# Cross-shaped window attention: the tiles that were scored twice become 16-bit words in three phases, and the work order is new

## Chip, core and metric

One NeuronCore of a Trainium2 chip runs the whole kernel. The metric is device time in microseconds (us); the time of the kernel before is the median of 3 runs, 1017.18 us (1016.98 to 1017.32). Engines are named as in the profile: PE is TensorE (matmul, with PEld its weight loads), ACT is ScalarE, DVE is VectorE, POOL is GpSimd, SP issues most DMAs.

## The reference

```python
qkv = jnp.einsum('bhwc,cd->bhwd', x, wqkv)          # x: 1 x 224 x 224 x 96
# first 48 channels: 28 horizontal windows of 8 x 224 = 1792 tokens
ah = _softmax(jnp.einsum('bqc,bkc->bqk', qh, kh) * scale, axis=-1)
oh = jnp.einsum('bqk,bkc->bqc', ah, vh)
# last 48 channels: the same over 28 vertical windows of 224 x 8 tokens
...
return jnp.einsum('bhwc,cd->bhwd', o, wo)           # o: both halves side by side
```

So there are 56 windows, each with 1792 x 1792 scores, and one exp for each score.

## The kernel before

**Tiling.** The windows go in 28 pairs P (14 horizontal, then 14 vertical). A pair has four chunks c of 512, 512, 512 and 256 queries, and 14 key blocks of 128. One tile is 128 keys x 512 queries of both windows of the pair, so 128x1024 scores in two PSUM banks; in the chunk of 256 queries two key blocks share a tile. That makes 49 tiles for each pair and 1372 in all. A tile is scored on PE (`qk_fn`, L670, or `s_fn`, L683), turned into exp(score) in one of the bf16 buffers `PT`, and then summed over its keys against V by PE (`pv_fn`, L696), which adds all tiles of a chunk up in one PSUM bank. A column of ones in V gives the softmax sum with it.

**Who makes the exp.** Most tiles go to ACT, one ACTIVATE each (L888). The rest, `p_seq`, is computed without ACT, in one of three ways, which a backlog rule in `step_dve` picks (L1189, L1190):

- *whole*: DVE copies the scores to an f32 buffer `qb` (L1191). POOL then takes four steps over it (L1108 to L1111).
- *stay*: three DVE passes over the scores, which stay in PSUM (L1192, L1205, L1213). POOL does nothing.
- *scored twice*: DVE makes a factor in `qb` (L1192) and gives the PSUM banks back; POOL squares it into `PT` (L1105); later PE scores the tile a second time and DVE adds the square to these scores (L1213).

**Other work.** PE projects K, Q and V of the next pair in small fills (L435, L481, L463) that DVE evicts; DVE takes each finished chunk out of PSUM (L1166); PE multiplies it by wo (L530, L566); DVE divides by the softmax sum (L537, L545, L573, L580), and in the vertical half POOL adds the stored horizontal part (L584), or DVE does both in one (L593). SP sends the rows out.

**What sets the order.** A planner in the kernel (`Sched`, `step_pe`, `step_dve`, `step_pool`) runs once in Python with fixed durations and writes down one instruction list for each engine. On the chip each engine works through its list in order and waits on semaphores. Rules by pair and chunk (`HOW`) say how many of a chunk's tiles leave ACT and how PE groups its work. ACT scores come from two PSUM sets (`SETS`), and from the third when the p tiles leave it free, so PE can be about one tile ahead of ACT. PE works in two modes: scores and output fills (mode A), and PV and projection fills (mode B); `pe_switch` counts a cost for each change. There are 16 `PT` and 6 `qb` buffers.

Of the kernel before, what the change touches and what calls it, by code (L numbers as in the profile page):

```python
# [8 lines left out]
U16 = mybir.dt.uint16  # L9
ACTF = mybir.ActivationFunctionType  # L10
# [6 lines left out]
SOFF = 140.0  # L17
# [3 lines left out]
NPT = 16  # L21
NQB = 6
# [9 lines left out]
D_TS, D_TW = 1.125, 1.28  # L32
L_SQ, L_TS, L_TW, LATE_TS = 1.96, 1.145, 1.43, 0.13
# [9 lines left out]
HOW = [  # L43
    ("032", 6, "2953291003432 2653291003432 2653291013432 3653291013434"),
    ("333", 11, "3653391013234 3653391013234 5684191017241 5664191017243"),
    ("344", 7, "5664181027243 5664181027243 5664181028223 5681181025223"),
    ("444", 6, "5681181025223 5681180025223 5681180025223 5681180025223"),
    ("444", 2, "3764140021423 3764240021423 3764260121423 5764260121223"),
    ("333", 11, "2382160013403 2382360013443 2a24191028322 2a24191028323"),
    ("333", 1, "2a24191018323 2a24191018333 3a24191008133 3824191008133"),  # L50
    ("333", 10, "3824191018333 3824190018333 3874190018433 3874190028433"),
    ("443", 4, "3874190028440 3874190028440 3853190028430 3853191024430"),
    ("434", 12, "3833191024430 3833191020230 3833191020230 3832191020240"),
    ("325", 5, "5852251021313 2721171113121 2413281038423 2413281009423"),
    ("444", 2, "4413281009431 4413281019131 4813281029131 5324251019342"),
    ("313", 11, "4a63260030213 4994190008032 3462191002341 3162191002341"),
    ("524", 12, "4562191002341 4562191006441 4563191006143 2a23170011403"),
    ("534", 0, "2a23170011401 3a23170011411 3a23170011414 3a23270116414"),
    ("433", 2, "5942160006420 2973160008411 2973160008441 2973160008441"),
    ("334", 10, "2593341023304 2914380019334 4643191009032 2412280129443"),  # L60
    ("233", 8, "2083141038412 3811171010220 5613180028441 4433381011434"),
    ("444", 4, "5722161037443 5722191037443 5724191027443 5724191024444"),
    ("333", 5, "5724191020404 3a82181025434 3a82181025414 4a82181025434"),
    ("334", 11, "4a12161025431 4a12161025231 4a12161125214 3a11161125214"),
    ("444", 11, "5764190008424 5764191008424 5764191008421 5764191018420"),
    ("533", 11, "5764191018430 5764191017430 5764191037430 5761191033430"),
    ("333", 11, "5761191035430 2263191205441 5673280004431 5473280004434"),
    ("334", 6, "5463280034444 3973340009320 4954180009121 4954180009121"),
    ("333", 7, "4954180005141 4954180005121 4954181005121 4954181005124"),
    ("434", 3, "4954181005123 2424150226241 2424150036241 2424151036211"),  # L70
    ("434", 6, "5743180003230 3961260009412 2241270105112 2241270000112"),
]
OFF = [[int(d) for d in k] + [0] for k, _, _ in HOW]
TAIL = [t for _, t, _ in HOW]
RULES = [[[int(d, 16) for d in r[:8]] + [(0.0, 0.03, 0.06, 0.1)[int(r[8])]] + [int(d) for d in r[9:]] for r in rs.split()] for _, _, rs in HOW]
# [3 lines left out]
class Sched:  # L79
# [13 lines left out]
    def deps(self, eng, reads, writes):  # L93
        d = set()
        for k in reads:
            for s, v in self.wr.get(k, {}).items():
                if not (s == eng and eng == "pe"):
                    d.add((s, v))
        for k in writes:
            if k[0] != "out":  # L100
                for s, v in self.wr.get(k, {}).items():
                    if not (s == eng and eng == "pe"):
                        d.add((s, v))
            for s, v in self.rd.get(k, {}).items():
                if s != eng or k[0] == "rc":
                    d.add((s, v))
        return d
# [56 lines left out]
def bass_standalone__window_attn_cswin__vision_kernel(  # L164
# [15 lines left out]
    NCH = 4  # L180
# [11 lines left out]
    with es:  # L192
# [23 lines left out]
        PT = [sb(f"PT{i}", [128, 1024], BF16) for i in range(NPT)]  # L216
# [65 lines left out]
        KC = [4.8125 / 128.0, 21.0]  # L282
        QC = [60.0, 32.0]
# [50 lines left out]
        pool_now(["one"], lambda e: e.memset(one_sb[:], 1.0), 0.12)  # L334
        pool_now(["woz"], lambda e: e.memset(woh[:], 0.0), 0.2)
# [278 lines left out]
        def dve_commit(item, t):  # L614
# [18 lines left out]
        tiles = {}  # L633
        act_seq, p_seq = [], []
        pv_left = {}
        for P in range(NP):
            for c in range(NCH):
                sz = CH_SIZES[c]
                step = 512 // sz
                groups = [list(range(k, k + step)) for k in range(0, NKT, step)]  # L640
                off = OFF[P][c]
                na = len(groups) - off
                for i, kts in enumerate(groups):
                    t = dict(P=P, c=c, kts=kts, q0=CH_Q0[c], qs=sz, kind="A" if i < na else "P")
                    tiles[(P, c, i)] = t
                    (act_seq if i < na else p_seq).append(t)
                pv_left[(P, c)] = len(groups)
# [41 lines left out]
        def pv_fn(t, slot, st, sp_, pb):  # L689
            b = t["P"] % 2  # L690

            def fn(e):
                for i, kt in enumerate(t["kts"]):
                    for w in range(2):
                        ca = w * 512 + i * t["qs"]
                        ins = e.matmul(bank(pb)[64 * w:64 * w + CA, 0:t["qs"]], lhsT=V_sb[b][:, w, kt, :],  # L696
# [19 lines left out]
        s2_q = []  # L716
        s1_q = []
# [94 lines left out]
        def queue_prep(P):  # L812
# [4 lines left out]
            a0 = pair_act0[P - 1]  # L817
            n = pair_act0[P] - a0 if P < NP else 0
# [5 lines left out]
        pair_act0 = {}  # L824
        for i, t in enumerate(act_seq):
            pair_act0.setdefault(t["P"], i)
# [53 lines left out]
        def issue_qka(t, s):  # L880
            tl = act_seq[ia[0]]
            slot = slot_free.pop(0)
# [6 lines left out]
                PT[slot][:], ps[:, 512 * SETS[s]:512 * SETS[s] + 1024], ACTF.Exp, scale=LN2 / 128.0),  # L889
                set_keys(s), pt_keys(slot), fresh=pt_keys(slot))  # L890
            pv_ready[(tl["P"], tl["c"])].append((tl, slot))
# [13 lines left out]
        def v_keys(b):  # L905
            return [("V", b, k0) for k0 in range(0, 2 * NKT, VS)] + ["vones"]

        def pv_cands(t):
# [12 lines left out]
            for it in pv_ready[pc]:  # L921
                tl, slot = it
                rt = S.ready("pe", pt_keys(slot) + v_keys(P % 2), [], LATE)
# [3 lines left out]

        def issue_pv(it, t):
            tl, slot = it
# [3 lines left out]
            if first:  # L933
# [7 lines left out]
            S.commit("pe", t, D_MM, L_PV, pv_fn(tl, slot, first, last, pb),  # L941
                     pt_keys(slot) + v_keys(b), [("bank", pb)],
# [3 lines left out]
            slot_free.append(slot)  # L946
            if tl["kind"] != "A":
# [6 lines left out]

        def p_before(i, tl):
            return (p_seq[i]["P"], p_seq[i]["c"]) <= (tl["P"], tl["c"])

        def how():
            tl = act_seq[min(ia[0], len(act_seq) - 1)]
            return RULES[tl["P"]][tl["c"]]  # L960

# [3 lines left out]
        def step_pe():  # L965
# [8 lines left out]
            def p_wants():  # L974
                return bool(s2_q and s2_q[0]["ready"] <= t + 0.2) or (n_mid() <= PBACK and p_open())

            def p_open():
                if ip[0] >= len(p_seq) or not qb_free or p_ahead[0] >= PAHEAD or not slot_free:
                    return False
                tl = p_seq[ip[0]]  # L980
# [381 lines left out]
```

## Time and profile before

| | |
|---|---|
| median of 3 runs | 1017.18 us |
| profiled execution, first to last instruction | 1015.7 us |
| ACT busy | 1004.9 us (99%) |
| PE busy (ends modelled) | 977.0 us (96%) |
| DVE busy | 956.6 us (94%) |
| POOL busy | 930.7 us (92%) |
| granted PE clock | 1.000 |

The profiled execution has no other time of its own than the span; the median of the runs is 1.5 us above it, which lies before the first and after the last instruction. In a list of groups, a line reads: line of the kernel, engine, operation, output <- input, shapes, count | busy us in all, mean ns of one | idle time ahead of it and what ended that. In a timeline: start us, duration us, engine, line, operation, count.

### The profile page before, as it was taken

What the parts mean: (1) busy time and instruction counts of PE and PEld (TensorE: products, weight loads), DVE (VectorE), ACT (ScalarE), POOL (GpSimd) and SP (SyncE); (2) the same over time, 40 slices, a digit from 0 to 9 for tenths busy, and PEclk for the clock granted to TensorE, in tenths of its full rate; (3) what the DMA queues carried; (4) which work ended last, traced back from release to release, by engine and by line L of the source; (5) the groups of instructions that cost most, each with busy time, mean ns of one, the idle gap of its engine ahead of it and who ended that gap; (6) DMA issues with size and microseconds to landing.
All of it is one profiled execution on the core that took longest, in us unless ns stands there. A gap on an engine that the chain in (4) does not pass through costs nothing.

```text
span 1015.7 us, 30751 instructions
## 1 busy us (share of the span) xinstructions
PE 977.0 (96%) x13367; PEld 392.0 (39%) x13367; DVE 956.6 (94%) x1468; ACT 1004.9 (99%) x1101; POOL 930.7 (92%) x717
## 2 busy tenths in 40 slices
PE   9999999999999999999999999999999999999997
PEld 4433434443433334333343433333433343343333
DVE  7989999999999999999999999999999999999997
ACT  8999999999999999999999999999999999999997
POOL 5999999989999998999999898999999999999995
PEclk9999999999999999999999999999999999999999
DMA  3222303202220320222022133122312213312111
GB/s 87 62 65 65 63 17 66 66 18 62 66 65 2 79 65 8 60 39 38 1 39 48 26 59 56 26 51 58 59 22 61 48 20 61 52 36 58 20 23 34
DMA packets 162873, 47.02 MB, mean 46 GB/s; under 512 B 155895, under 2 KB 162711, under 8 KB 162738
## 3 DMA queue, kind: packets, MB, share of 16 engines
q1 hardware_dynamic: 161618, 44.57, 22.0%
q8 instruction: 104, 1.70, 0.7%
q10 hardware_dynamic: 1120, 0.49, 0.2%
q14 instruction: 31, 0.25, 0.1%
HBM read 10.60 MB, written 19.28 MB: 29 GB/s over the span
## 4 chain that ended last, share of the span: by engine, by line
ACT 99%; PE 1%; DVE 0%; issue 0%; DVEq 0%
ACT PT L888 99%; PE ps L346 0%; PE ps L731 0%; DVE out_all L593 0%; ACT xT_sb L747 0%; DVE OT_sb L1166 0%; PE ps L696 0%; PE ps L670 0%; DVE warm L309 0%; DVEq L192 0%; PE ps L753 0%; DVE rc L573 0%; DVE scr L310 0%
## 5 line engine op out<-in xcount | busy, mean ns | idle before, releaser
L888 ACT ACTIVATE PT<-ps 128x1024 bf16<-128x1024 f32 x1090 | 1000.5, 1094 | 1.1 <-PE ps L670 1.1
L670 PE MATMUL ps<-QT_sb,KT_sb 49*64 49x512 bf16 (+1 forms) x5144 | 447.4, 363 | 31.0 <-ACT PT L888 17.0
L696 PE MATMUL ps<-PT,V_sb 128*49 128x512 bf16 (+1 forms) x3136 | 456.2, 361 | 0.9 <-ACT PT L888 0.5
L670 PEld LDWEIGHTS ps<-QT_sb,KT_sb 49*64 49x64 bf16 x5144 | 129.8, 103 | 374.3 <-ACT PT L888 355.5
L1109 POOL TENSOR_TENSOR PT<-PT 128x1024 f16<-128x1024 f16 x138 | 261.4, 1894 | 9.8
L1110 POOL TENSOR_SCALAR qb<-PT 128x1024 uint16<-128x1024 f16 x138 | 186.2, 1349 | 12.0
L696 PEld LDWEIGHTS ps<-PT,V_sb 128*49 128x49 bf16 x3136 | 133.6, 103 | 163.8 <-issue 131.6
L1192 DVE TENSOR_SCALAR qb<-ps 128x1024 f32<-128x1024 uint16 x144 | 175.9, 1222 | 7.2 <-PE ps L683 5.4
L1213 DVE SCALAR_TENSOR_TENSOR PT<-ps,PT 128x1024 uint16<-128x1024 bf16 x144 | 175.7, 1220 | 5.6 <-PE ps L683 5.1
L1191 DVE COPY qb<-ps 128x1024 f32<-128x1024 f32 x138 | 168.6, 1222 | 11.5 <-PE ps L683 10.3
L1108 POOL TENSOR_SCALAR PT<-qb 128x1024 f16<-128x1024 uint16 x138 | 144.5, 1047 | 33.7 <-DVE qb L1191 23.8
L1111 POOL TENSOR_SCALAR PT<-qb 128x1024 uint16<-128x1024 f32 x138 | 144.5, 1047 | 11.2
L683 PE MATMUL ps<-QT_sb,KT_sb 50*64 50x512 bf16 x1376 | 136.0, 385 | 1.7 <-DVE qb L1192 0.4
L1105 POOL TENSOR_TENSOR PT<-qb 128x1024 f16<-128x1024 f32 x62 | 116.0, 1894 | 1.0
L1205 DVE SCALAR_TENSOR_TENSOR PT<-ps,qb 128x1024 f16<-128x1024 uint16 x82 | 100.0, 1219 | 0.1
L584 POOL TENSOR_TENSOR out_all<-tmp,Ph_sb 128x480 bf16<-128x480 f32 (+1 forms) x73 | 74.4, 1032 | 3.3 <-DVE tmp L580 1.6
L1166 DVE CAST OT_sb<-ps 113x512 bf16<-113x512 f32 x112 | 69.3, 618 | 6.1 <-PE ps L696 5.4
L451 DVE CAST QT_sb<-ps 128x512 bf16<-128x512 f32 (+1 forms) x111 | 68.1, 616 | 5.1 <-PE ps L435 4.5
L440 DVE TENSOR_SCALAR_CACHE_REDUCE KT_sb<-ps 128x512 bf16<-128x512 f32 x108 | 66.3, 616 | 3.2 <-PE ps L435 2.5
L545 DVE TENSOR_TENSOR Ph_sb<-ps,rc 128x480 bf16<-128x480 f32 (+1 forms) x84 | 52.2, 621 | 2.0
L488 DVE CAST V_sb<-ps 128x480 bf16<-128x480 f32 (+1 forms) x84 | 51.9, 620 | 2.2 <-PE ps L481 1.7
L683 PEld LDWEIGHTS ps<-QT_sb,KT_sb 50*64 50x64 bf16 x1376 | 39.2, 104 | 31.1 <-DVE PT L1213 9.6
(64 smaller groups left out, 444.5 us busy)
## 6 DMA issues: line engine op xcount, KB each, us to landing
cols_dram<-in_x_dram SPq DMA_DIRECT2D x28, 336.0 KB
out_dram<-out_all SPq DMA_DIRECT2D x386, 24.0 KB, 1.9
xT_sb<-cols_dram SPq DMA_TRANSPOSE x28, 4.8
xT_sb<-in_x_dram SPq DMA_TRANSPOSE x26, 4.7
xT_sb<-ones_dram SPq DMA_DIRECT2D x26, 7.0 KB
Ph_sb<-in_x_dram SPq DMA_DIRECT2D x2, 168.0 KB, 3.5
Ph_sb<-in_x_dram ACTq DMA_DIRECT2D x2, 168.0 KB, 3.7
out_dram<-out_all ACTq DMA_DIRECT2D x6, 24.0 KB, 1.9
```

The costliest lines, as they stand in the source:

```text
L670: ins = e.matmul(bank(SETS[s] + w)[64 * kh:64 * kh + 64, i * t["qs"]:(i + 1) * t["qs"]], lhsT=KT_sb[b][64 * w:64 * w + CA, kt * 128 + 64 * ...
L683: ins = e.matmul(bank(PB0 + w)[64 * kh:64 * kh + 64, 0:512], lhsT=KT_sb[b][64 * w:64 * w + nr, kt * 128 + 64 * kh:kt * 128 + 64 * kh + 64] ...
L696: ins = e.matmul(bank(pb)[64 * w:64 * w + CA, 0:t["qs"]], lhsT=V_sb[b][:, w, kt, :], rhs=PT[slot][:, ca:ca + t["qs"]], start=st and i == 0 ...
L888: S.commit("act", 0.0, D_ACT, None, lambda e, s=s, slot=slot: e.activation(PT[slot][:], ps[:, 512 * SETS[s]:512 * SETS[s] + 1024], ACTF.Ex ...
L1105: return [("pool", (D_SQ, L_SQ, 0.0), lambda e: e.tensor_tensor(y, q, q, ALU.mult), qk, yk)]
L1108: return [("pool", (D_TS, L_TS, LATE_TS), lambda e: e.tensor_scalar(y, lo, 2.0 ** -16, QH, ALU.mult, ALU.add), qk, yk), ("pool", (D_SQ, L_ ...
L1109: ("pool", (D_SQ, L_SQ, 0.0), lambda e: e.tensor_tensor(y, y, y, ALU.mult), yk + ["pser"], yk),
L1110: ("pool", (D_TW, L_TW, LATE_TS), lambda e: e.tensor_scalar(lo, y, 65536.0 * P2, 65536.0 * QC0, ALU.mult, ALU.add), yk + ["pser"], [("q", ...
L1111: ("pool", (D_TS, L_TS, LATE_TS), lambda e: e.tensor_scalar(bits, q, 1.0, 128.0 * (127.0 - SOFF), ALU.mult, ALU.add), qk, yk)]
L1191: S.commit("dve", t, D_P1, D_P1 + SEMD, lambda e: e.tensor_copy(qb[tl["qb"]][:], ps[:, PB0 * 512:(PB0 + 2) * 512]) if tl["whole"] else e.t ...
L1192: qb[tl["qb"]][:], ps[:, PB0 * 512:(PB0 + 2) * 512]) if tl["whole"] else e.tensor_scalar(
L1213: S.commit("dve", t, D_P1, D_P1 + SEMD, lambda e: e.scalar_tensor_tensor(PT[tl["slot"]][:].bitcast(U16), half(BF16, 1), 128.0 * (127.0 - S ...
```

## The change

Tiles are no longer scored twice. The tiles that do not go to ACT now have a written kind, by pair and chunk, in `TYPES`: `w` (the four POOL steps as before, the last one now a plain copy that converts), `s` (the three DVE passes as before), and the new `p`. The rows of `TYPES` hold 124 `w`, 95 `p` and 81 `s`. For a `p` tile:

- PE scores it once. The scores carry the factor 128, so that as a 16-bit word they are the bits of a bf16 number, which rises in straight pieces between powers of two.
- DVE makes these words in one pass over PSUM, straight into a `PT` buffer (it adds a constant and converts).
- POOL makes two more tiles from it in one step: it reads pairs of words as int32 and adds 42 or 85 to each word, so the straight pieces are shifted by a third and two thirds of an octave.
- PE sums all three tiles, the two shifted ones against copies of V scaled by 0.793 and 0.637 (`VB_sb`, made by POOL, two small steps for each pair, for the last three key blocks alone).

So a `p` tile takes three `PT` buffers and three PV groups. There are 25 `PT` and 4 `qb` buffers now. All rules of the order are new (`HOW`: one for each half of a chunk's ACT tiles). The core of the diff:

```diff
-NPT = 16
-NQB = 6
+NPT = 25
+NQB = 4
...
-    ("032", 6, "2953291003432 2653291003432 2653291013432 3653291013434"),
+wps pwsp wwsp
+wws pwsp wwps
...
-        KC = [4.8125 / 128.0, 21.0]
-        QC = [60.0, 32.0]
+        KC = [4.8125 / 128.0, 4.8125]
+        QC = [1728.0, 127.0]
...
+            if g[0] == "V" and all(("V", g[1], k0) in flags for k0 in range(0, 2 * NKT, VS)):
+                b = g[1] % 2
+                for j in range(2):
+                    pool_q.append(dict(what="vb", P=g[1], j=j, reads=[("V", b, k0) for k0 in range(0, 2 * NKT, VS)] + ["vones", "pser"], writes=[("VB", b)],
+                                       fn=lambda e, b=b, j=j: e.tensor_scalar(VB_sb[b][:, j, :, :, :], V_sb[b][:, :, NKT - KPH:NKT, :], PH_W[j], None, ALU.mult)))
...
+            pv_left[(P, c)] = n + 2 * (len(kinds) - late)
...
-                        ins = e.matmul(bank(pb)[64 * w:64 * w + CA, 0:t["qs"]], lhsT=V_sb[b][:, w, kt, :],
+                        ins = e.matmul(bank(pb)[64 * w:64 * w + CA, 0:t["qs"]], lhsT=VB_sb[b][:, ph - 1, w, kt - (NKT - KPH), :] if ph else V_sb[b][:, w, kt, :],
...
-            if not tl["whole"]:
-                return [("pool", (D_SQ, L_SQ, 0.0), lambda e: e.tensor_tensor(y, q, q, ALU.mult), qk, yk)]
+            if tl["kind"] == "p":
+                a, b, c = tl["slots"]
+                words = PT_all[:, :, :].rearrange("p s n -> p (s n)").bitcast(I32).rearrange("p (s n) -> p s n", s=NPT)
+                return [("pool", (D_SQ, L_SQ, 0.0), lambda e: e.tensor_tensor(
+                    words[:, b:c + 1:c - b, :], words[:, a:a + 1, :].to_broadcast([128, 2, 512]),
+                    kph[:, :].unsqueeze(2).to_broadcast([128, 2, 512]), ALU.add), pt_keys(a) + ["pser"], pt_keys(b) + pt_keys(c))]
...
-                    ("pool", (D_TS, L_TS, LATE_TS), lambda e: e.tensor_scalar(bits, q, 1.0, 128.0 * (127.0 - SOFF), ALU.mult, ALU.add), qk, yk)]
+                    ("pool", (D_TS, L_TS, LATE_TS), lambda e: e.tensor_copy(bits, q), qk, yk)]
...
-                rt = S.ready("dve", pt_keys(tl["slot"]), [])
-                s2_q.append(dict(t=tl, ready=rt - 0.5))
...
+                if kind == "p":
+                    fn = lambda e: e.tensor_scalar(PT[tl["slot"]].bitcast(U16), sc, -PH_OFF, None, ALU.add)
+                elif kind == "w":
+                    fn = lambda e: e.tensor_copy(qb[tl["qb"]][:], sc)
```

How the instruction lists change, counted from both:

| engine | what | before | now |
|---|---|---|---|
| ACT | exp of a tile | 1090 | 1072 |
| PE | score groups for tiles off ACT | 344 | 300 |
| PE | PV groups of one tile | 1372 | 1562 |
| PE | changes from mode A to mode B | 773 | 896 |
| DVE | passes over 128x1024 | 508 | 462 |
| DVE | output in one (128x96) / by way of POOL | 53 / 73 | 185 / 45 |
| POOL | whole tiles, four steps each | 138 | 124 |
| POOL | squares / phase steps | 62 / 0 | 0 / 95 |
| POOL | output adds / steps for the scaled V | 73 / 0 | 45 / 56 |

The other fills, evictions and DMAs are the same in number. PE's list near the middle of the program, where chunks of a horizontal pair run, stood as follows (L670 scores for ACT, L683 scores for a tile off ACT, L696 PV, L530 an output fill; four score matmuls or two PV matmuls are one tile):

```order
L670 MATMUL ps<-QT_sb,KT_sb 64x512 x4
L683 MATMUL ps<-QT_sb,KT_sb 64x512 x4
L670 MATMUL ps<-QT_sb,KT_sb 64x512 x4
L530 MATMUL ps<-woh,OT_sb 64x97 x10
L696 MATMUL ps<-PT,V_sb 49x512 x4
L670 MATMUL ps<-QT_sb,KT_sb 64x512 x4
L683 MATMUL ps<-QT_sb,KT_sb 64x512 x4
L670 MATMUL ps<-QT_sb,KT_sb 64x512 x4
```

Now a like place, with the PV groups of a `p` tile in it (L728 scores for ACT, L754 PV, L472 a projection fill), reads:

```order
L728 MATMUL ps<-QT_sb,KT_sb 64x512 x4
L754 MATMUL ps<-PT_all,V_sb 49x512 x2
L754 MATMUL ps<-PT_all,VB_sb 49x512 x2
L728 MATMUL ps<-QT_sb,KT_sb 64x512 x4
L754 MATMUL ps<-PT_all,VB_sb 49x512 x2
L472 MATMUL ps<-xT_sb,wq_sb 64x512 x2
L754 MATMUL ps<-PT_all,V_sb 49x512 x2
L728 MATMUL ps<-QT_sb,KT_sb 64x512 x4
```

What moved: the score group of a tile off ACT stood between two ACT score groups without a change of mode; where PV groups took its place, nearly every ACT score group stands alone between two changes.

POOL's list in the early part stood so (L1108 to L1111 the four steps of a whole tile, L1105 the squares):

```order
L1109 TENSOR_TENSOR PT<-PT 128x1024
L1105 TENSOR_TENSOR PT<-qb 128x1024 x3
L1110 TENSOR_SCALAR qb<-PT 128x1024
L1111 TENSOR_SCALAR PT<-qb 128x1024
L1108 TENSOR_SCALAR PT<-qb 128x1024
```

Now, at a like place (L1184 to L1187 the four steps, L1176 the phase step, with `kph` the two constants):

```order
L1185 TENSOR_TENSOR PT_all<-PT_all 128x1024
L1176 TENSOR_TENSOR PT_all<-PT_all,kph 128x2x512
L1186 TENSOR_SCALAR qb<-PT_all 128x1024
L1176 TENSOR_TENSOR PT_all<-PT_all,kph 128x2x512
L1187 CAST PT_all<-qb 128x1024
L1184 TENSOR_SCALAR PT_all<-qb 128x1024
```

What moved: the squares, which came in runs, are gone, and phase steps stand between the four steps of the whole tiles.

More of the change, by code (lines that the diff above doesn't have):

```diff
@@ L9 @@
 U16 = mybir.dt.uint16
+I32 = mybir.dt.int32
 ACTF = mybir.ActivationFunctionType
@@ L73 @@
-OFF = [[int(d) for d in k] + [0] for k, _, _ in HOW]
-TAIL = [t for _, t, _ in HOW]
-RULES = [[[int(d, 16) for d in r[:8]] + [(0.0, 0.03, 0.06, 0.1)[int(r[8])]] + [int(d) for d in r[9:]] for r in rs.split()] for _, _, rs in HOW]
+TYPES = """
+wps pwsp wwsp
+wws pwsp wwps
+wws wpsp pwws
+wsw wpsp pwws
+wsw wpsp pwws
+wsw wpsp pwws
+wsw wpsp pwws
+wsw wpsp pwws
+wsw wpsp pwws
+wsw wpsp pwws
+wsw wpsp pwws
+wp wwspp pwss
+wp wwspp wwss
+wp wwspp wwss
+wp wwspp wwss
+wp pwwspp wss
+wp pwwspp wss
+w pwwpsp wss
@@ L634, in bass_standalone__window_attn_cswin__vision_kernel @@
         act_seq, p_seq = [], []
         pv_left = {}
[L636 to L647, printed above, removed]
+        GROUPS = [NKT, NKT, NKT, NKT // 2]
@@ new lines, in bass_standalone__window_attn_cswin__vision_kernel, with add_chunk @@
+        POS0 = [0, NKT, 2 * NKT, 3 * NKT]
+        NPOS = sum(GROUPS)
+        def add_chunk(P, c):
+            sz = CH_SIZES[c]
+            step = 512 // sz
+            kinds = OFFS[P][c]
+            assert step == 1 or not kinds
+            left = [list(range(k, k + step)) for k in range(0, NKT, step)]
+            n = len(left)
+            na = n - len(kinds)
+            late = sum(z != "p" for z in kinds)
+            rest = left[na:]
+            for z in kinds:
+                if z == "p":
+                    kts = rest.pop()
+                    assert kts[0] >= NKT - KPH
+                else:
+                    kts = rest.pop(0)
+                p_seq.append(dict(P=P, c=c, kts=kts, q0=CH_Q0[c], qs=sz, kind=z))
+            for i in range(na):
+                act_seq.append(dict(P=P, c=c, kts=left[i], q0=CH_Q0[c], qs=sz, kind="A",
+                                    pos=P * NPOS + POS0[c] + i * n / na, seg=2 * (4 * P + c) + (2 * i >= na), first=i == 0))
+            pv_left[(P, c)] = n + 2 * (len(kinds) - late)
```

246 lines of the change are left out of this document (141 added, 105 removed).

## Prediction

> **What bounds the kernel now.** I read the busy shares first, then the chain that ended last, then the waits, since four engines are above 90%.
>
> ```profile
> PE 977.0 (96%) x13367; PEld 392.0 (39%) x13367; DVE 956.6 (94%) x1468; ACT 1004.9 (99%) x1101; POOL 930.7 (92%) x717
> ```
>
> The shares alone name no bound. The chain in order of time does:
>
> ```profile
> 9.07 0.37 PE ps L670 x4
> 9.44 0.02 issue
> 9.46 810.43 ACT PT L888 x883
> 819.89 0.02 issue
> 819.91 190.05 ACT PT L888 x207
> 1009.96 0.04 issue
> ```
>
> From 9.46 to 1009.96 us the end is set by one exp after the other: 810.43 + 190.05 = 1000.5 us for 883 + 207 = 1090 tiles. The group and the waits say the same from the other side:
>
> ```profile
> L888 ACT ACTIVATE PT<-ps 128x1024 bf16<-128x1024 f32 x1090 | 1000.5, 1094 | 1.1 <-PE ps L670 1.1
> ```
> ```profile
> PEld ps L670 <- ACT PT L888: 355.5, 926, 0.8
> ```
>
> One exp costs 1000.5 / 1090 = **0.918 us** (the mean of 1094 ns counts the overlap with the next). ACT waited 1.1 us in all for scores, while PE's loads of score weights waited 926 times for ACT to give a PSUM set back. So a tile taken off ACT is worth 0.918 us, as long as the others keep ACT fed.
>
> **ACT's term.** The rows of `TYPES` leave ACT 1072 tiles instead of 1090: 18 x 0.918 = **16.5 us** less. The exp itself keeps its shape and its operands. The head (9.46 us) and the tail (1015.7 - 1009.96 = 5.7 us) keep their steps but for a few output rows; I take both as unchanged. With ACT never idle the span is 9.46 + 1072 x 0.918 + 5.7 = 999.2 us, and with the 1.5 us by which the median of the runs is above the span, 1000.7 us. The question is what the other three engines make of it.
>
> **PE's term.** Matmul ends are modelled, so I count from start to start, in stretches without a wait:
>
> ```profile
> 502.59 0.41 PE L670 MATMUL ps<-QT_sb,KT_sb 49*64 49x512 bf16 x4
> 502.83 0.39 PE L683 MATMUL ps<-QT_sb,KT_sb 50*64 50x512 bf16 x4
> ...
> 503.56 0.39 PE L530 MATMUL ps<-woh,OT_sb 49*64 49x97 bf16 x10
> 503.88 0.62 PE L696 MATMUL ps<-PT,V_sb 128*49 128x512 bf16 x4
> 504.43 0.41 PE L670 MATMUL ps<-QT_sb,KT_sb 49*64 49x512 bf16 x4
> 504.77 0.62 PE L696 MATMUL ps<-PT,V_sb 128*49 128x512 bf16 x4
> 505.31 0.41 PE L670 MATMUL ps<-QT_sb,KT_sb 49*64 49x256 bf16 x8
> ...
> 506.55 0.40 PE L696 MATMUL ps<-PT,V_sb 128*49 128x512 bf16 x2
> 506.78 0.38 PE L435 MATMUL ps<-xT_sb,wq_sb 97*64 97x512 bf16 x2
> 507.10 0.41 PE L670 MATMUL ps<-QT_sb,KT_sb 49*64 49x256 bf16 x8
> ```
>
> Score to score takes 0.24 us (502.59 to 502.83), score to PV 0.34: a change of mode costs 0.10. Two PV tiles and the way back take 0.54 (504.77 to 505.31), one PV tile alone about 0.22 (0.23 from 506.55 to 506.78), so the way back costs 0.10 too. A projection fill is 0.22 (506.78 to 507.10 less the change), an output fill of ten matmuls also 0.22 (503.56 to 503.88 less the change). A V fill is 0.31:
>
> ```profile
> 140.43 0.48 PE L481 MATMUL ps<-w_sb,xT_sb 96*64 96x48 bf16 x20
> 140.74 0.38 PE L696 MATMUL ps<-PT,V_sb 128*49 128x512 bf16 x2
> ```
>
> Before: 1434 score groups x 0.24 + 1372 PV x 0.22 + 773 pairs of changes x 0.20 = 801 us, and the fills about 104 (K and Q 168 x 0.22 and 56 halves, output 157 x 0.22, V 78 x 0.31): 905 us, 90% of the 1000.5 in which the exps run. After: 62 fewer score groups (-14.9), 190 more PV (+41.8), 123 more pairs of changes (+24.6): **956 us, or 97%** of 984. PE's cover shrinks from 95 to 28 us. As PE can be no more than about one tile ahead, what counts is the local load. I walk through both lists with these durations. In the old order 2 of 1071 stretches of 20 ACT tiles ask more than the 18.36 us that ACT takes for them, the worst 18.45; in the new order 49 of 1053 do, the worst 19.03. A score group must have ended (0.41 us) before ACT is through with the other set (0.918), so PE may be late by 0.4 to 0.5 us before ACT notices. Summing what goes over that reserve gives 0 in the old order, as the trace has it, and 2.7 to 4.2 us in the new; with a reserve of only 0.3 it gives 7. Bounds 0 and 7; I take **3.5 us**, in the middle of the sums nearest to the trace.
>
> **DVE's term.** All passes over a tile cost alike:
>
> ```profile
> L1192 DVE TENSOR_SCALAR qb<-ps 128x1024 f32<-128x1024 uint16 x144 | 175.9, 1222 | 7.2 <-PE ps L683 5.4
> L1213 DVE SCALAR_TENSOR_TENSOR PT<-ps,PT 128x1024 uint16<-128x1024 bf16 x144 | 175.7, 1220 | 5.6 <-PE ps L683 5.1
> L1191 DVE COPY qb<-ps 128x1024 f32<-128x1024 f32 x138 | 168.6, 1222 | 11.5 <-PE ps L683 10.3
> ...
> L593 DVE SCALAR_TENSOR_TENSOR out_all<-ps,rc,Ph_sb 128x96 bf16<-128x96 f32 x53 | 13.0, 311 | 0.3
> ```
> ```profile
> 703.83 0.66 DVE L580 TENSOR_TENSOR tmp<-ps,rc 128x480 f32<-128x480 f32 x1
> 704.41 1.21 DVE L1191 COPY qb<-ps 128x1024 f32<-128x1024 f32 x1
> 705.54 0.16 DVE L467 TENSOR_REDUCE wq_sb<-ps 96x2 bf16<-96x8 f32 x1
> ```
>
> A pass occupies 1.13 us (704.41 to 705.54), and f32, 16-bit, one or two operands are the same within 2 ns. So the new pass, f32 scores to 16-bit words, is priced the same, from these rows; its bounds are half and twice that, -54 to +107 us for 95. There are 46 fewer passes: -52 us. Of the output, 28 tiles of scaled rows fewer at about 0.58 (703.83 to 704.41) are -16, and 132 more one-row steps at 13.0/53 = 0.245 are +32. Sum -36: busy 921 us, 92% of the span. DVE gets looser, at the twice price it would not (1028).
>
> **POOL's term.**
>
> ```profile
> L1109 POOL TENSOR_TENSOR PT<-PT 128x1024 f16<-128x1024 f16 x138 | 261.4, 1894 | 9.8
> L1110 POOL TENSOR_SCALAR qb<-PT 128x1024 uint16<-128x1024 f16 x138 | 186.2, 1349 | 12.0
> L1108 POOL TENSOR_SCALAR PT<-qb 128x1024 f16<-128x1024 uint16 x138 | 144.5, 1047 | 33.7 <-DVE qb L1191 23.8 <-DVE rc L573 0.4
> L1111 POOL TENSOR_SCALAR PT<-qb 128x1024 uint16<-128x1024 f32 x138 | 144.5, 1047 | 11.2
> L1105 POOL TENSOR_TENSOR PT<-qb 128x1024 f16<-128x1024 f32 x62 | 116.0, 1894 | 1.0
> L584 POOL TENSOR_TENSOR out_all<-tmp,Ph_sb 128x480 bf16<-128x480 f32 x47 | 51.1, 1097 | 2.2 <-DVE tmp L580 1.0
> L319 POOL COPY wq_sb<-wst 96x96 bf16<-96x96 bf16 x4 | 1.1, 264 | 0.2
> L327 POOL COPY w_sb<-wst 96x192 bf16<-96x192 bf16 x1 | 0.3, 341 | 1.7 <-DMA wst<-in_wqkv_dram 1.7
> ```
>
> A whole tile is 1.894 + 1.349 + 2 x 1.047 = 5.34 us busy; 14 fewer are -75. The 62 squares go, -116; 28 adds go, -29. Two copies, 264 ns for 96 elements and 341 for 192, give 0.8 ns an element: 1.0 us for 1024, so the converting copy in place of L1111 is priced at L1111's 1.05; and 0.42 for the 294 of a scaled V: 56 x 0.42 = +24. The unknown is the phase step, int32 words, 1024 results, two inputs, one of them read twice. No row has int32. Two-input steps take 1.894 with f16 and with f32 inputs alike, which speaks for the element count as the price. Bounds: 1.05, as a one-input pass of 1024, and 3.79, as if each of the 2048 16-bit words were an element. I take 1.9, the row nearest in count and inputs: 95 x 1.9 = +180. Sum -16: 915 us busy. The gaps between POOL's steps come on top (idle ahead of L1109, L1110 and L1111 is 33 us for 414 steps, 0.08 each; with L1108, less the 24 us in which it waits for DVE, some 45 to 50 us in all): before 930.7 + 50 = 981, after about 915 + 48 = 963 us, **96% of the span** as before. So POOL has little to spare, and the phase step decides.
>
> The Trainium skill (GPSIMD Engine Reference, section 3.1) gives a two-input elementwise step on GpSimd about 2.6 cycles an element at 1.2 GHz. That would be an estimated 2.2 us for 1024 elements, 29 us more in 95 steps; the trace has 1.894 for both two-input rows, so by the trace the page's figure is too high here, and whether int32 behaves as f32 does no run shows.
>
> What the change adds in waits: PV of the two shifted tiles waits for POOL, and behind it in PE's list stand ACT's next scores. DVE's pass for a `p` tile frees the score banks after 1.13 us, where a scored-twice tile took them twice; that is in DVE's favour. DMAs are the same in number.
>
> **The sum.** 9.46 + 984.0 + 3.5 + 5.7 = 1002.7 us of span, and 1.5 outside: **1004 us**.
>
> **Rivals.**
>
> 1. *ACT stays fed*: the order has PE lean just where ACT has a tile in hand. For it: 1.1 us of waiting in 1000 now, with POOL as full. Against it: 97% of PE. It gives 1000.7 us.
> 2. *PE is held by POOL*: a phase step of 2.2 us brings POOL to 991 us with its gaps, 99% of the span. Each of the 95 then lands late for a PV group whose successors are ACT's scores; if a third of the 0.3 us excess passes ACT's reserve it costs 95 x 0.1 = 10 us: 1010 to 1015 us. For it: one or two phase steps stand between the steps of whole tiles, so their results come late too.
> 3. *POOL becomes the bound, and the kernel slower*: without phase steps POOL's sum is 963 - 180 = 783 us; with a step of x us, 783 + 95x. It passes the 1000.5 us that the exps take now at x = 2.3, and since POOL then sets the end, the time is above 1017 from about there (head and tail as they are). At the upper bound, 3.79, it is 1143 + 15 + 1.5 = 1160 us. For it: int32 is in no row, and the output is 4 bytes wide. Against it: f32 input of 4 bytes costs nothing over f16.
>
> **How the numbers follow.** Forecast (some PE stalls, 1002.5 to 1009) 0.43; rival 1 (999.5 to 1002.5) 0.27; rival 2 (1009 to 1015) 0.13; between that and no change within 0.2%, 1015.1 to 1019.2, which is about what a measurement of this kernel can tell, 0.05; rival 3 0.12. Faster is 0.43 + 0.27 + 0.13 = 0.83. The range takes in the forecast, rival 1 and most of rival 2: 999.5 to 1014, which holds 0.81. PE's bounds (0 and 7 us of stalls) lie in it; the upper bounds of DVE's pass and POOL's step are what is left out.
>
> **What would show it.** Right: 1072 exps at 0.918 us; idle ahead of them of 2 to 7 us, ended by PE's scores; far fewer waits of PE's score weights for ACT than 355 us; phase steps near 1.9 us; DVE busy near 921. Wrong: a phase step above 2.2 us, POOL without idle time and PE's PV waiting for it (rival 2 or 3); or ACT idle above 10 us with POOL on time, which would mean that changes of mode cost more in the new order than 0.20 a pair.

## The result and the profile after

The changed kernel takes **1008.38 us** (median of 4 runs, 1008.03 to 1008.55), against 1017.08 us (1016.88 to 1017.32, 4 runs) for the kernel before. The ratio is 0.9914, 95% interval 0.9900 to 0.9928. It is faster by 8.7 us; the prediction was 1004 us, a gain of 13.

The busy shares and the chain that ended last, by engine, of the changed kernel:

```profile
span 1006.8 us, 30979 instructions
...
PE 991.3 (98%) x13488; PEld 392.2 (39%) x13488; DVE 921.3 (92%) x1526; ACT 992.5 (99%) x1083; POOL 935.9 (93%) x724
...
ACT 53%; POOL 33%; PE 10%; DVE 2%; issue 1%; DVEq 0%
```

Again the shares of ACT and PE look like the bound, and POOL's 93% like nothing. The chain says something else: a third of it is POOL. The groups of the steps that the prediction priced (busy us, mean ns of one, idle ahead of it):

```profile
L951 ACT ACTIVATE PT_all<-ps 128x1024 bf16<-128x1024 f32 x1072 | 988.0, 1062 | 3.7 <-PE ps L728 2.7
...
L1176 POOL TENSOR_TENSOR PT_all<-PT_all,kph 128x1024 int32<-128x1024 int32 x95 | 178.5, 1892 | 4.5 <-DVE PT_all L1268 3.3
...
L1187 POOL CAST PT_all<-qb 128x1024 uint16<-128x1024 f32 x124 | 128.5, 1037 | 5.2
L1268 DVE TENSOR_SCALAR PT_all<-ps 128x1024 uint16<-128x1024 f32 x95 | 116.0, 1221 | 17.3 <-PE ps L741 16.1
...
L673 POOL TENSOR_SCALAR VB_sb<-V_sb 128x294 bf16<-128x294 bf16 x56 | 53.5, 956 | 4.7 <-DVE V_sb L525 0.8
```

Four of the five came in at the price given. The scaled V did not: 956 ns instead of 420. The chain in order of time shows where the time is:

```profile
209.09 3.71 POOL PT_all L1176 x2
...
244.41 3.71 POOL PT_all L1176 x2
...
350.40 3.71 POOL PT_all L1176 x2
...
362.82 1.34 POOL qb L1186
369.25 29.54 ACT PT_all L951 x32
...
431.50 415.60 ACT PT_all L951 x452
```

From about 48 us to 364 POOL sets the pace but for short breaks (one near 136 us), and again for much of the stretch from 867 to 931. From 369 us on it is mostly ACT, and from 431.50 to 847.10 ACT is alone on the chain. The pairs of phase steps in the first stretch come every 35.32 us (209.09 to 244.41; four times to 350.40, 35.33 in the mean), once for each pair of windows. ACT's busy time and exps in one such period:

```profile
209.09:244.41 35.32, 35.20 (x39) 1.00 0.25 58
```

The 39 count one exp cut in two by the edges, so 38 to a pair: 38 x 0.918 = 34.88 us. POOL needs 0.45 us more for a pair than ACT does. ACT still looks busy for 35.2 of 35.3 us: in the kernel before an exp's record is 1094 ns long and the next one starts 918 ns after it, so the records overlap, and an exp that waits up to about 0.18 us (1094 - 918 ns) shows no idle time. The lost time stands in the mean, not in the idle column: 988.0 / 1072 = 0.9216 us an exp, where the kernel before had 0.918. In the period from 209 us the chain shows POOL at work without a hole but the 0.05 to 0.08 us between steps, and both scaling steps of the pair are on it:

```profile
222.84 0.08 issue
222.92 0.95 POOL VB_sb L673
223.87 1.00 POOL PT_all L1187
224.87 0.07 issue
224.95 0.95 POOL VB_sb L673
```

At 0.42 us each they would make the period 35.33 - 2 x 0.53 = 34.27 us, under ACT's 34.88. PE's list shows how the delay reaches ACT. One PV group waits for the step L1187 that stands behind the first scaling step and ends at 224.87, and ACT's next scores (L728) come behind this group:

```profile
224.92 0.62 PE L754 MATMUL ps<-PT_all,V_sb 128*49 128x512 bf16 x6 [0.25 <-POOL PT_all L1187]
225.47 0.41 PE L728 MATMUL ps<-QT_sb,KT_sb 49*64 49x512 bf16 x4
```

From the first exp's start to the last one's end it is 1000.19 - 9.61 = 990.6 us in the changed kernel:

```profile
9.61 2.85 ACT PT_all L951 x3
...
1000.19 0.04 issue
```

That is 6.6 us over the 984.0 of an ACT that is always fed. The prediction had 3.5 for it. So of the 4.1 us by which the span (1006.8) exceeds the forecast one (1002.7), 3.1 lie here, 0.9 in the tail (6.6 us instead of 5.7; the last DVE step on the chain ends 4.1 us before the end of the span instead of 2.8, so it is the landing of the last rows that takes longer) and 0.15 in the head.

### The profile page after: what moved, and what is told of

It reads as the page before. It is cut to its first block, busy times and chain, and to the rows that moved or that the text cites. A ratio compares the mean times of both kernels' runs of the same rounds, so it can differ in the third digit from the quotient of the medians.

```text
span 1006.8 us, 30979 instructions
## 1 busy us (share of the span) xinstructions
PE 991.3 (98%) x13488; PEld 392.2 (39%) x13488; DVE 921.3 (92%) x1526; ACT 992.5 (99%) x1083; POOL 935.9 (93%) x724
## 4 chain that ended last, share of the span: by engine, by line
ACT 53%; POOL 33%; PE 10%; DVE 2%; issue 1%; DVEq 0%
ACT PT_all L951 53%; POOL PT_all L1185 9%; POOL qb L1186 6%; POOL PT_all L1176 5%; POOL PT_all L1184 5%; POOL PT_all L1187 5%; PE ps L754 4%; PE ps L728 3%; POOL VB_sb L673 2%; PE ps L741 1%; PE ps L472 0%; PE ps L383 0%; POOL out_all L621 0%; PE ps L787 0%; PE ps L518 0%
## 5 line engine op out<-in xcount | busy, mean ns | idle before, releaser
L951 ACT ACTIVATE PT_all<-ps 128x1024 bf16<-128x1024 f32 x1072 | 988.0, 1062 | 3.7 <-PE ps L728 2.7
L754 PE MATMUL ps<-PT_all,V_sb 128*49 128x512 bf16 (+1 forms) x3136 | 445.4, 360 | 3.6 <-POOL PT_all L1187 3.5
L728 PE MATMUL ps<-QT_sb,KT_sb 49*64 49x512 bf16 (+1 forms) x5072 | 438.1, 363 | 5.1 <-ACT PT_all L951 0.9
L728 PEld LDWEIGHTS ps<-QT_sb,KT_sb 49*64 49x64 bf16 x5072 | 127.4, 103 | 337.4 <-ACT PT_all L951 306.2
L1185 POOL TENSOR_TENSOR PT_all<-PT_all 128x1024 f16<-128x1024 f16 x124 | 234.7, 1892 | 5.3
L754 PEld LDWEIGHTS ps<-PT_all,V_sb 128*49 128x49 bf16 x3136 | 131.3, 103 | 157.2 <-issue 118.0
L1176 POOL TENSOR_TENSOR PT_all<-PT_all,kph 128x1024 int32<-128x1024 int32 x95 | 178.5, 1892 | 4.5 <-DVE PT_all L1268 3.3
L1186 POOL TENSOR_SCALAR qb<-PT_all 128x1024 uint16<-128x1024 f16 x124 | 166.9, 1346 | 10.7
L1270 DVE COPY qb<-ps 128x1024 f32<-128x1024 f32 x124 | 151.6, 1223 | 19.0 <-PE ps L741 16.3
L1184 POOL TENSOR_SCALAR PT_all<-qb 128x1024 f16<-128x1024 uint16 x124 | 129.5, 1044 | 21.9 <-DVE qb L1270 12.0
L1187 POOL CAST PT_all<-qb 128x1024 uint16<-128x1024 f32 x124 | 128.5, 1037 | 5.2
L1268 DVE TENSOR_SCALAR PT_all<-ps 128x1024 uint16<-128x1024 f32 x95 | 116.0, 1221 | 17.3 <-PE ps L741 16.1
L1285 DVE SCALAR_TENSOR_TENSOR PT_all<-ps,qb 128x1024 f16<-128x1024 uint16 x81 | 98.6, 1217 | 0.1
L1293 DVE SCALAR_TENSOR_TENSOR PT_all<-ps,PT_all 128x1024 uint16<-128x1024 bf16 x81 | 98.5, 1216 | 0.0
L754 PE MATMUL ps<-PT_all,VB_sb 128*49 128x512 bf16 x380 | 66.5, 387 | 0.0
```

What stands on the lines that cost most here:

```text
L728: ins = e.matmul(bank(SETS[s] + w)[64 * kh:64 * kh + 64, i * t["qs"]:(i + 1) * t["qs"]], lhsT=KT_sb[b][64 * w:64 * w + CA, kt * 128 + 64 * ...
L951: S.commit("act", 0.0, D_ACT, None, lambda e, s=s, slot=slot: e.activation(PT[slot], ps[:, 512 * SETS[s]:512 * SETS[s] + 1024], ACTF.Exp, ...
L1176: return [("pool", (D_SQ, L_SQ, 0.0), lambda e: e.tensor_tensor(words[:, b:c + 1:c - b, :], words[:, a:a + 1, :].to_broadcast([128, 2, 512 ...
L1184: return [("pool", (D_TS, L_TS, LATE_TS), lambda e: e.tensor_scalar(y, lo, 2.0 ** -16, QH, ALU.mult, ALU.add), qk, yk), ("pool", (D_SQ, L_ ...
L1185: ("pool", (D_SQ, L_SQ, 0.0), lambda e: e.tensor_tensor(y, y, y, ALU.mult), yk + ["pser"], yk),
L1186: ("pool", (D_TW, L_TW, LATE_TS), lambda e: e.tensor_scalar(lo, y, 65536.0 * P2, 65536.0 * QC0, ALU.mult, ALU.add), yk + ["pser"], [("q", ...
```

## The experiments

Theory after the result: the scaled V, at 956 ns, makes POOL's list longer than ACT's by 0.45 us for each pair in the first half, and this is most of the 3.1. Rival A: the loss is PE's load of 97% (the prediction's own term, mis-sized). Rival B: POOL is late for another reason, such as the order in which phase steps and whole tiles alternate.

### 1. vb_tiny: the scaling step on two elements

```diff
-fn=lambda e, b=b, j=j: e.tensor_scalar(VB_sb[b][:, j, :, :, :], V_sb[b][:, :, NKT - KPH:NKT, :], PH_W[j], None, ALU.mult)
+fn=lambda e, b=b, j=j: e.tensor_scalar(VB_sb[b][:, j, 0, 0, 0:2], V_sb[b][:, 0, NKT - KPH, 0:2], PH_W[j], None, ALU.mult)
```

`VB_sb` is filled once with a constant, so V is not scaled. The three lists of PE, DVE and ACT stay the same.

> The two steps per pair that scale V work on 2 elements instead of 294; all lists stay in the same order. What is left out: V is not scaled for the shifted tiles, they are summed against a constant set once. Theory (these steps, at 0.956 us instead of the 0.42 us of the sum, fill POOL and hold back PE and so ACT): the steps fall to 0.1 to 0.2 us, POOL is idle for some 40 us more, ACT's loss of 7.7 us goes nearly away, 1001 to 1003 us. Rival (PE at 97% with its changes of mode is what ACT waits for): 1007 to 1009 us, as now.

Median 1007.7 us, ratio 0.9890 (0.9876 to 0.9905). But the five runs are of two kinds: 1003.47 and 1003.86 us, and 1007.70, 1007.78 and 1007.84. The profiled run is one of the second kind, and in it the PE clock falls, which the profile of the kernel before doesn't show (us of the window, busy us of PE, PEld, DVE, ACT and POOL, then the granted clock):

```profile
12.00:14.00 2.00, 1.67 (x32) 0.67 (x28) 1.99 (x3) 2.00 (x3) 1.22 (x2) 1.00 0.03 7
14.00:16.00 2.00, 1.66 (x14) 0.43 (x12) 1.42 (x3) 2.00 (x3) 2.00 (x2) 0.58 0.07 7
16.00:18.00 2.00, 2.00 (x14) 0.42 (x12) 2.00 (x3) 1.11 (x2) 1.92 (x3) 0.50 0.09 14
...
24.00:26.00 2.00, 2.00 (x22) 0.56 (x20) 0.90 (x1) 1.59 (x3) 0.00 (x0) 0.86 1.62 132
```

For some 10 us the clock is at a half and ACT is fed slowly (1.11 of 2 us busy). That is the 4 us between the two kinds. POOL's share of the chain is gone even in this run (ACT 97%, PE 2%). The two runs without the fall, 1003.5 and 1003.9, are 4.5 to 4.9 us under the changed kernel, a little above the 1001 to 1003 of the expectation. This speaks for the theory and against rival A as the whole of the loss. Of rival B it says that the order alone isn't the cause: the same order with a shorter step loses nothing to POOL. The clock is a matter of its own (experiment 7).

### 2. vb_forms: why the step takes 956 ns

One kernel, in which the 56 steps take seven forms in turn by pair (copy; one contiguous row; 48 columns instead of 49; f32 output; f16; multiply and add 0.0; as it is). It leaves the scaling right only where the form does.

```diff
+            if k == 1:
+                return e.tensor_copy(dst, src)
...
+            if k == 6:
+                return e.tensor_scalar(dst, src, PH_W[j], 0.0, ALU.mult, ALU.add)
+            return e.tensor_scalar(dst, src, PH_W[j], None, ALU.mult)
```

> One look. The step that scales V takes another form in each pair (pair number modulo 7): 0 and 6 as it is and with an added zero, 1 a plain copy of the same shape, 2 a multiply of 294 elements in one row, 3 the same shape with 48 columns instead of 49, 4 one row with f32 output, 5 one row with f16 in and out. V is wrong in all but 0 and 6. If the shape (two rows, odd width) costs, forms 2, 4 and 5 take about 0.42 us and form 3 is lower; if the bf16 arithmetic costs, forms 1 and 5 take about 0.42 and forms 2 and 3 about 0.95; if it is a fixed cost of the step, all take about 0.95.

The groups, eight steps of each form:

```profile
L668 POOL TENSOR_SCALAR vb_f<-V_sb 128x294 f32<-128x294 bf16 x8 | 7.7, 963 | 0.6
L673 POOL TENSOR_SCALAR VB_sb<-V_sb 128x294 bf16<-128x294 bf16 x8 | 7.7, 961 | 0.5
L670 POOL TENSOR_SCALAR vb_h<-V_sb 128x294 f16<-128x294 f16 x8 | 7.7, 957 | 0.8 <-DVE V_sb L527 0.3
L664 POOL TENSOR_SCALAR VB_sb<-V_sb 128x294 bf16<-128x294 bf16 x8 | 7.7, 956 | 0.7
L666 POOL TENSOR_SCALAR VB_sb<-V_sb 128x288 bf16<-128x288 bf16 x8 | 7.5, 941 | 0.6
L672 POOL TENSOR_SCALAR VB_sb<-V_sb 128x294 bf16<-128x294 bf16 x8 | 3.6, 445 | 0.7
L662 POOL COPY VB_sb<-V_sb 128x294 bf16<-128x294 bf16 x8 | 3.5, 437 | 0.4 <-DVE V_sb L527 0.4
```

Type and layout change nothing, and one column fewer (L666) takes 941 ns for 288 elements. What matters is the number of operations: with one (multiply, no second operation) the step on 294 elements takes 956 to 963 ns, with two (multiply, then add 0.0; L672) 445, a copy (L662) 437. A one-operation form other than the multiplication was not run on POOL. None of the causes I had named was right, but the run had the answer in it. The price from copy rows, 420, was nearly that of a copy and of a two-operation step; it was wrong for this form alone. No POOL row of before had the one-operation form. On DVE's passes over PSUM it costs nothing: the new one has one operation too (an addition) and takes 1221 ns, as the passes with two. The one run of this kernel, with 16 of the 56 steps short, took 1007.44 us, between the changed kernel and vb_two below.

### 3. vb_two: the same kernel with the two-operation form

```diff
-PH_W[j], None, ALU.mult)
+PH_W[j], 0.0, ALU.mult, ALU.add)
```

> The step that scales V is written as multiply and add of zero instead of multiply alone; the value, the lists and their order are the same. Theory (POOL's surplus of 0.5 us in each of 56 steps is what holds back ACT beyond PE's load): the step takes 0.445 us, POOL has 28 us less to do, no stretch of the chain of waits stays on POOL for long, 1003 to 1004.5 us. Rival (ACT's loss is PE's alone): 1007 to 1009 us.

Ratio 0.9889 (0.9871 to 0.9907) over all five runs, median **1003.74 us**. Three runs lie at 1003.71 to 1003.74, two at 1007.8 with the clock's fall. The chain and the groups of one at 1003.74:

```profile
span 1001.9 us, 30979 instructions
...
PE 990.0 (99%) x13488; PEld 391.7 (39%) x13488; DVE 920.2 (92%) x1526; ACT 990.4 (99%) x1083; POOL 907.8 (91%) x724
...
ACT 98%; PE 1%; DVE 0%; issue 0%; DVEq 0%
...
L951 ACT ACTIVATE PT_all<-ps 128x1024 bf16<-128x1024 f32 x1072 | 986.2, 1064 | 1.2 <-PE ps L728 1.1
```

POOL goes from 33% of the chain to nothing that shows, on 28 us less busy time (935.9 to 907.8). From the first exp's start to the last one's end it is now 986.3 us:

```profile
9.06 37.74 ACT PT_all L951 x41
...
995.38 0.04 issue
```

995.38 - 9.06 = 986.3, 4.3 us less than in the changed kernel, from 56 steps of 0.51 us less each. 28 us off POOL buy 4.3, since POOL's list was only 0.45 us a pair over ACT's and only in part of the program; the rest is room. Set side by side by their number, the exps of the changed kernel fall 2.9 us behind those of vb_two by about 450 us, nothing more until 887, and 1.4 between 887 and 957. So two thirds of the 4.3 belong to the stretch read above, and a third to the short one near the end. The version is faster than both kernels.

### 4 and 5. vb_told and vb_dve: let the planner know, or move the step

vb_told gives the planner the measured duration (and nothing else), vb_dve gives the step to DVE. In both the planner writes a new order.

```diff
-D_TS, D_TW, D_VB = 1.125, 1.28, 0.4
-L_SQ, L_TS, L_TW, L_VB, LATE_TS = 1.96, 1.145, 1.43, 0.52, 0.13
+D_TS, D_TW, D_VB = 1.125, 1.28, 1.0
+L_SQ, L_TS, L_TW, L_VB, LATE_TS = 1.96, 1.145, 1.43, 1.1, 0.13
```

> The planner is told 1.0 us for the step that scales V instead of 0.4, and writes a new order by its rules; the work is the same. Theory (POOL has too much work per pair in the first half): 1005 to 1010 us, since 35.3 us of POOL per pair stay. Rival (only the surprise costs, a right plan hides it): 1001 to 1004 us.

```diff
-                    pool_q.append(dict(what="vb", P=g[1], j=j, reads=[("V", b, k0) for k0 in range(0, 2 * NKT, VS)] + ["vones", "pser"], writes=[("VB", b)],
+                    dve_q.append(dict(what="vb", P=g[1], j=j, reads=[("V", b, k0) for k0 in range(0, 2 * NKT, VS)] + ["vones"], writes=[("VB", b)],
```

> The steps that scale V go to DVE, 0.3 us assumed each; the planner writes a new order. Theory: POOL loses 53 us, DVE gains about 17 us and stays near 93%: 1001 to 1004 us. Rival (PE's changes of mode): 1007 to 1010 us. A third case: DVE's step from buffer to buffer collides with POOL's steps and lengthens them; then POOL's groups show longer means.

vb_told: 1078.38 us (1071.15 to 1078.43), ratio 1.059 (1.057 to 1.061). vb_dve: six runs from 1070.98, the profiled one, to 1099.96; the three below 1083 us give a ratio of 1.061 (1.059 to 1.063). Theory and rival of both missed by 60 us or more. The exps of vb_told, and its windows before and in its worst stretch (busy us of PE, PEld, DVE, ACT, POOL, then the granted clock):

```profile
L951 ACT ACTIVATE PT_all<-ps 128x1024 bf16<-128x1024 f32 x1072 | 995.8, 1060 | 63.4 <-PE ps L728 61.7
```
```profile
750.00:800.00 50.00, 49.24 (x654) 18.54 (x648) 44.16 (x82) 50.00 (x56) 44.98 (x34) 1.00 0.22 44
...
850.00:900.00 50.00, 47.61 (x470) 16.09 (x470) 32.07 (x59) 33.42 (x35) 28.75 (x22) 0.62 0.16 34
...
950.00:1000.00 50.00, 45.11 (x588) 19.90 (x584) 36.83 (x71) 43.86 (x48) 39.47 (x30) 1.00 0.20 38
```

ACT waits 62 us for PE's scores. About half of its idle time falls between 800 and 950 us, where the granted clock is low (0.62 in the second window, ACT busy 33 of 50 us); the rest stands in windows at or near the full clock, as in the third (ACT busy 43.86 of 50). The rules by pair and chunk (`HOW`) were fitted to one plan; a plan that runs 0.6 us later on POOL takes other decisions with the same rules. That its order feeds ACT badly shows at the full clock; which of its decisions does it, and whether it also brings the low clock, was not followed up. So these two runs say nothing on the price of the step, only that this order could not be re-planned with one number changed. The third case of vb_dve did not come as written: POOL's steps keep their means (1892, 1346, 1044 and 1036 ns), and it is the step on DVE that grows, to 641 ns in the mean where 0.3 us was assumed. What vb_dve shows of the step on DVE stands in the last section.

### 6. pv_short: how much of the rest is PE

vb_two, with the PV of the shifted tiles on 64 of 512 columns, except where it opens or closes a chunk; so part of the sum is left out.

```diff
+                        nq = 64 if ph and not st and not sp_ else t["qs"]
...
-                                       rhs=PT[slot][:, ca:ca + t["qs"]],
+                                       rhs=PT[slot][:, ca:ca + nq],
```

> As vb_two, and the PV groups of the shifted tiles sum 64 of the 512 columns (unless they open or close their chunk). What is left out: the sum over the shifted tiles for the other columns. Theory (what is left above 1000.7 us is PE's load of 97%): PE has some 32 us less to do, 1000.5 to 1001.5 us. Rival (what is left is POOL's or DVE's): 1003 to 1004.5 us, as vb_two.

Two runs with the full clock: 1002.38 and 1002.57 us, two with its fall 1006.43 and 1006.48; ratio 0.9876 (0.9859 to 0.9893). Against vb_two's 1003.7 that is 1.2 us, less than expected. Both runs lie between the two ranges expected. PE's load thus accounts for about 1.2 of the 2.3 us by which vb_two's exps (986.3) exceed 984.0; where the other 1.1 are, I did not settle.

### 7. head_fill, head_fill2, later_fill: the clock's fall

In the three kernels vb_tiny, vb_two and pv_short 7 of 14 runs had the clock's fall. Two of the seven, one of vb_tiny and one of pv_short, are profiled; the other five are told by their times, some 4 us longer, and a mean granted clock of 0.993 or 0.994. PE's timeline of the profiled vb_tiny has two short holes just ahead of it (the last column is idle time and its releaser):

```profile
12.51 0.41 PE L730 MATMUL ps<-QT_sb,KT_sb 49*64 49x512 bf16 x4 [0.23 <-ACT PT_all L953]
...
13.60 0.41 PE L730 MATMUL ps<-QT_sb,KT_sb 49*64 49x512 bf16 x4
14.34 0.64 PE L730 MATMUL ps<-QT_sb,KT_sb 49*64 49x512 bf16 x4 [0.34 <-ACT PT_all L953]
```

The group at 14.34 is the first slow one (0.64 us instead of 0.41). But the profiled run of vb_two, at the full clock in this stretch, has the same two holes:

```profile
12.88 0.41 PE L728 MATMUL ps<-QT_sb,KT_sb 49*64 49x512 bf16 x4 [0.23 <-ACT PT_all L951]
...
14.72 0.41 PE L728 MATMUL ps<-QT_sb,KT_sb 49*64 49x512 bf16 x4 [0.34 <-ACT PT_all L951]
```

So the holes alone don't bring the fall. To see whether they are needed for it, I filled the holes with warm matmuls in the first pair's V fills, and as a control put the same matmuls into the second pair's:

```diff
                 def pe_fn(e, bk, k0=k0, n=n):
+                    for _ in range(1 if P == 0 else 0):
+                        e.matmul(bk[0:64, 0:512], lhsT=warm[:, 0:64], rhs=warm[:, 0:512], start=True, stop=True)
```

(head_fill2: two of them; later_fill: `P == 1`.)

> The two-operation VB step, and ahead of each of the three V fills of the first pair one more warm matmul of 512 columns (about 0.2 us each) into the same PSUM bank. In 7 of 14 runs of the three timed variants so far the granted PE clock fell to a half from about 14 to 25 us, at a cost of about 4.1 us; PE waits for ACT there, 0.23 us at 12.65 and 0.34 us at 14.38. Theory (PE's gaps there make the clock fall): no run, or one at most, at 1007.8; all near 1003.7. Rival (it is something else, such as what the chip did before the kernel): 2 or 3 of 5 runs at 1007.8 as before.

> The same with two warm matmuls ahead of each of the three V fills. Theory: no run at 1007.8, all near 1003.7 to 1004.0 (the second matmul may delay a score by up to 0.2 us, once or twice). Rival: 2 or 3 of 5 runs at 1007.8.

> Control: the same three extra matmuls ahead of the V fills of the second pair instead, where the clock never fell. Theory and rival alike: 2 or 3 of 5 runs at 1007.8, the others at 1003.7 to 1004.0.

head_fill 1004.17 us (1003.95 to 1004.48), head_fill2 1004.75 (1004.17 to 1004.82), later_fill 1004.36 (1004.24 to 1004.65), ratios 0.9873, 0.9877 and 0.9875, each within 0.0017. No run of the 12 shows the fall, the four of the control included, which has the holes as they were; its forecast of 2 or 3 missed as well. So the theory is not borne out: what the control does without, the filling can't be credited with. These 12 runs were on a third chip; the seven falls had come on two others (three with vb_tiny on one, four with vb_two and pv_short on the other). The changed kernel's own four runs had none either. Whether it is the chip or chance stays open. The three medians are 0.4 to 1.0 us above vb_two's 1003.7, so nothing was gained by the filling.

## Why the prediction was right, and where its size was off

The direction, the range and the mechanism "ACT's 18 tiles less, minus what the others keep" hold; the gain is 8.7 us where 13 were forecast. That 1008.4 falls into the stretch given to the forecast (some PE stalls, 1002.5 to 1009) is in part luck: of the 6.6 us that the exps lost, 4.3 came from POOL, which is the way of rival 2. Point by point:

- **ACT's term** (1072 exps at 0.918, -16.5 us): right. 1072 exps ran; in stretches where ACT is on the chain alone an exp still takes 0.9195 us (415.60 / 452). Head and tail "unchanged": the head was 0.15 us longer (it moves more than that from run to run: vb_two has 9.06 us, the changed kernel 9.61), the tail 0.9.
- **PE's term** (3.5 us of stalls, bounds 0 to 7): too high, and inside its bounds. With POOL out of the way (vb_two) the exps lose 2.3 us in all, of which the shorter PV gave back 1.2. So counting load in stretches of 20 tiles, with a reserve of 0.4 to 0.5 us, gave too much, by a factor of 1.5 to 3.
- **DVE's term** (busy 921): right to 0.3 us. The new pass took 1221 ns against the forecast 1.22 us.
- **POOL's term**, phase step at 1.9 us: right, 1892 ns, as the f16 row of the same kernel and within 2 ns of the f16 and f32 rows of before; int32 words and the doubled read cost nothing. By the rule of the Trainium skill (GPSIMD Engine Reference, section 3.1), an estimated 2.2 us, it would have been 0.3 us dearer; the measurement decides for the rows. The converting copy at 1.05: 1037 ns. **The scaled V at 0.42 us: wrong, and this is the mis-sized term.** It measured 956 ns, 56 x 0.54 = 30 us more on POOL than the sum had. The step was priced from copies, on the grounds that cost goes by elements. It was also not bounded from both sides, since it looked small. POOL's busy sum, forecast 915, was 935.9: of the difference of 21 the scaled V is 30, and the other steps together came in 9 lower.
- **"96% of the span as before, so the phase step decides"**: the right place, the wrong step. With the 45 to 50 us of gaps POOL was at 981 to 986 of 1006.8 us, 98%. In most of the horizontal half, where it needed 35.33 us for a pair, it decided.
- **The rivals.** Rival 1 (ACT stays fed, 1000.7) is not reached even with POOL out of the way. Rival 2 (PE held by POOL) is the mechanism that took most of the missing time, through another step than the one named. It is not the shifted tiles that come late (PE's loads for PV wait 1.5 us in all for phase steps) but whole tiles, whose last step (L1187) stands behind the scaled V. The loads of these PV groups wait 8.1 us, the matmuls 3.5 us; the 11 waits of the matmuls are also among the 15 of the loads. From 189 to 366 us they come once in each period of 35.3 us, and an exp feels only what passes ACT's reserve:

```profile
PEld ps L754 <- POOL PT_all L1187: 8.1, 15, 1.2
...
PE ps L754 <- POOL PT_all L1187: 3.5, 11, 0.9
```

  Rival 2's price, 10 us, was for 0.3 us on 95 steps; the real excess was 0.54 us on 56. That is about the same POOL time (28.5 and 30 us), and the real loss was 4.3 (2.9 by 450 us, 1.4 after 887), since only 0.45 us a pair stood above ACT's need, and only there. Rival 3 (POOL slower than everything) did not occur: its threshold was a phase step of 2.3 us.
- **The signs named ahead.** Idle time ahead of the exps of 2 to 7 us, ended by PE's scores: 3.7, of which 2.7 so. Phase steps near 1.9 and DVE near 921: both came. "Far fewer waits" of PE's score weights for ACT: no, they went from 355.5 to 306.2 us only:

```profile
PEld ps L728 <- ACT PT_all L951: 306.2, 838, 0.6
```

  And POOL without idle time, with PE's PV waiting for it, was a sign of rival 2; it came in the first half. The signs thus showed both at once, and only the experiments told their shares.

**The balance**: 1002.7 us of span forecast; +4.3 for the scaled V, -1.2 for PE's term (2.3 instead of 3.5), +1.05 for head and tail: 1006.85, against 1006.8 measured. It closes by construction, since the 4.3 and the 2.3 are both read from vb_two; the test of the cause is that experiment, not this sum. Of the 2.3 only the 1.2 of the shorter PV are shown to be PE's.

## What to carry to other kernels

Price every added step on a nearly full engine by a row of the same operation in the same form, and bound the small ones too: 56 steps at 0.5 us decided a third of the gain, because they took the engine from 0.6 us under the bounding one to 0.45 us over it in the pairs where it was fullest. Compare engines by the period of one piece of the program (35.33 against 34.88 us), not by shares of the span, and look for lost time in the mean spacing of the bounding steps, since short waits don't show as idle. Don't re-plan a fitted order to test one step; change the step in the same order.

## What the runs showed of the hardware beyond that

- **A multiplication alone costs more than one with an addition of zero on GpSimd.** A `tensor_scalar` that only multiplies 294 bf16 elements in each partition takes 956 ns, the same with a second operation that does nothing 445, a copy 437. On two elements the form that only multiplies takes 217 ns (median), so an estimate from these two points is 2.5 ns for each further element (739 ns / 292).
- **A DVE step can wait for whatever step POOL is in.** In vb_dve the 56 scaling steps on DVE (bf16, SBUF to SBUF) take 199 to 1574 ns. POOL's and DVE's timelines side by side:

```profile
48.51 1.89 POOL L1185 TENSOR_TENSOR PT_all<-PT_all 128x1024 f16<-128x1024 f16 x1
...
49.38 1.12 DVE L673 TENSOR_SCALAR VB_sb<-V_sb 128x294 bf16<-128x294 bf16 x1
```
```profile
17.18 0.80 DVE L673 TENSOR_SCALAR VB_sb<-V_sb 128x294 bf16<-128x294 bf16 x1
```
```profile
15.99 1.89 POOL L1176 TENSOR_TENSOR PT_all<-PT_all,kph 128x1024 int32<-128x1024 int32 x1
```

  The DVE step ends at 50.50, 0.10 us after POOL's (50.40), and at 17.98, 0.10 after POOL's 17.88. Of the 56 steps 44 end 0.09 to 0.10 us after the end of the POOL step that ran when they began; the other twelve, ten of which began while POOL was in no step, took 0.20 to 0.25. The Trainium skill (SBUF — State Buffer, Who interferes with whom) says that a DVE `tensor_scalar` in a two-port mode and a GpSimd instruction shut each other out, the one that began first keeping the ports to its end. The trace agrees where POOL began first (the 44 steps); whether the step was in such a mode, and the opposite order, no run here shows. DVE's passes over PSUM did not show it: 1216 to 1223 ns in vb_dve as in the changed kernel.
- **The clock's fall.** In the two profiled runs that show it PE's clock went to a half at about 14 us for some 10 us, behind holes of at most 0.34 us; five more of 14 runs of three kernels have the same loss of time. The Trainium skill (TensorE: Matmul & The Clock Gate, What's actually happening) ties it to an idle window of about 3.4 us; in these two runs the window of 2 us ahead of it (12 to 14) has PE busy for 1.67, so idle time of that length isn't there. The run of vb_two that keeps the full clock has 1.68 in the same window. What triggers it was not found.
